# An attention and MLP kernel whose MLP blocks grow from three token tiles to four, with a split at the start of a block

## The chip, the core and the metric

The kernel runs on one core of a Trainium2 chip. The metric is the device time of one execution in microseconds (us). Before the change it is 976.59 us, the median of three runs (975.79 to 978.5). The engines are PE (matmuls), DVE (VectorE), ACT (ScalarE), POOL (GpSimd) and SP, which here issues transfers.

## The reference

Eight batches of eight heads, 512 local and 32 global tokens of 64 numbers each. A global token attends to all 544, a local one to the 32 global tokens and to the local ones within 32 positions. The result, 4352 tokens of 512 numbers, goes through an MLP of 2048 hidden numbers, all in float32:

```
s_g = scale * q_g @ k_all.T;  out_g = sm(s_g) @ v_all
s_ll = where(|i - j| <= 32, scale * q_l @ k_l.T, -1e9)
a_l = sm(concat([scale * q_l @ k_g.T, s_ll]));  out_l = a_l @ concat([v_g, v_l])
x = concat([out_g, out_l]) as tokens x 512
h = x @ w_in;  g = h / (1 + exp(-h));  out = g @ w_out
```

## The kernel before

The tokens form 34 tiles of 128. An attention **step** is one of 128 pairs of heads with one of 32 local tiles: four steps make a tile. A step loads queries and keys (`st_load`, into one of two `raw` buffers), splits them into a high part in float32r and a rest (`st_split`: an ACT cast and two DVE subtractions), multiplies them (`st_scores`, L363 and L364 of the profile, four matmuls of 224 columns into one PSUM bank), takes the softmax on DVE and ACT, takes the halves of the words apart on POOL (`st_halves`, L393), sends them to DRAM (`st_away`, L398) and brings them back transposed (`st_back`, L402). SP issues its transfers in order, so a transpose that waits for its data in DRAM holds up what stands behind it. For four steps together, `st_out` (L444) multiplies with the values into two banks, and the result is split into `xh` and `xl`, 256 columns at a time. Per batch there are four pairs of global heads: `g_load`, `g_split`, `g_scores` (L272, L273: two banks; then an ACT copy, L274, and a DVE sum, L275), `g_soft`, and `g_turn` (L309, L312: transposes `gt` and `gu`, copied by ACT at L310 and L315).

The MLP takes the tiles in **blocks**, `SIZES`: ten of three tiles and two of two. For each of sixteen slices `f` of the hidden numbers, `first_layer` does twelve matmuls over all tokens of the block (`h`, L600), as `w_hi` with `xh`, `w_hi` with `xl`, `w_lo` with `xh`; then tanh (ACT, L607), a product (DVE, L608), a cast to `gh` (ACT, L610) and the rest `gl` (DVE, L611). `second_layer` for the slice before (L627) does three matmuls of 512 columns per tile into banks `out`, one bank for each tile.

Order: on PE it is written out. A list of attention pieces, each with a due time in units of steps (`DUE`, `DMAT`, `HEAD`, `TURN`, `VLOADS`), is sorted, and `fill` releases the pieces that are due while the MLP runs: after each first layer as many shares as the block has tiles, then one after every three matmuls of the second layer. During block n the attention of block n + 1 is done. On the other engines a scheduler orders the work at build time; instructions in `hold` keep the program's order.

PSUM has eight banks: two for `h`, three for `out`, and three through which scores, global scores, transposes and attention outputs rotate in turn (`attbank`). A bank is written again when the engines that read it have done so.

Of the kernel before, what the change touches and what calls it, by code (L numbers as in the profile page):

```python
# [38 lines left out]
SIZES = (3,) * 10 + (2, 2)  # L39
# [32 lines left out]
def attention_moe_kernel(ctx: ExitStack, tc: tile.TileContext, qk0_in, qk_in, v_in, gqk, wts, out):  # L72
# [16 lines left out]
    def attbank(kind, name):  # L89
        if early:  # L90
            i = next(banks[kind]) % {"s": 3, "t": 2, "o": 3}[kind]
            if i and kind == "s":
                return ps_h.tile([P, 512], F32, tag="h", name=name)
            if i:
                return ps_out.tile([P, 512], F32, tag="out2" if kind == "t" else f"out{i - 1}", name=name)
# [329 lines left out]
    def st_out(k0, n, b, c, t):  # L425
        blk, i = block_of[t]
        xh, xl = xtiles(blk)
# [18 lines left out]
        for i, o in enumerate(banks_):  # L446
            m = min(2, n)
            prs = slice(k0 % NPR + 2 * i, k0 % NPR + 2 * i + m)
            o = o[:, : m * wide].rearrange("p (r q) -> p r q", r=m)
            hi = xh[:, prs, sl]  # L450
            nc.scalar.copy(out=hi, in_=o[:, :, :P])
            nc.vector.tensor_tensor(out=xl[:, prs, sl], in0=o[:, :, :P], in1=hi.bitcast(F32), op=ALU.subtract)
            if k0 >= NPR:
                gdst = acc[:, prs, SG * (b % 4) : SG * (b % 4 + 1)]
                if c == 0 and k0 >= NST:
                    nc.vector.tensor_copy(out=gdst, in_=o[:, :, P:])
                else:
                    nc.vector.tensor_tensor(out=gdst, in0=o[:, :, P:], in1=gdst, op=ALU.add)
# [14 lines left out]
    def g_tile(t):  # L473
        n, i = block_of[t]
        xh, xl = xtiles(n)
        sl = slice(i * P, (i + 1) * P)
        nc.scalar.copy(out=xh[:, :, sl], in_=acc)
        nc.vector.tensor_tensor(out=xl[:, :, sl], in0=acc, in1=xh[:, :, sl].bitcast(F32), op=ALU.subtract)
# [23 lines left out]
    AHEAD = NPR  # L502
    for k, (t, b, c, pr) in enumerate(steps):
# [30 lines left out]
        put(at + due["load"], st_load, *a)  # L534
# [44 lines left out]
    def fill(part):  # L579
# [3 lines left out]
        total = NF * SIZES[n] + (NF - 1) * SIZES[n] + (SIZES[n - 1] if n else 0)  # L583
# [9 lines left out]
    def first_layer(n, f):  # L593
# [4 lines left out]
        for wt, x in ((w_hi[f], xh), (w_hi[f], xl), (w_lo[f], xh)):  # L598
            for c in range(NCC):
# [7 lines left out]
        nc.scalar.activation(t[:, :nt], h[:, :nt], AF.Tanh, scale=0.5)  # L607
        nc.vector.scalar_tensor_tensor(out=t[:, :nt], in0=t[:, :nt], scalar=1.0, in1=h[:, :nt], op0=ALU.add,  # L608
                                       op1=ALU.mult)
        nc.scalar.copy(out=gh[:, :nt], in_=t[:, :nt])  # L610
        nc.vector.tensor_tensor(out=gl[:, :nt], in0=t[:, :nt], in1=gh[:, :nt].bitcast(F32), op=ALU.subtract)  # L611
        return gh, gl

    def second_layer(n, f, gh, gl):
# [10 lines left out]
        for done_, (i, j) in enumerate(order_, 1):  # L625
# [26 lines left out]
    for n in range(len(SIZES)):  # L652
        for f in range(NF):
# [7 lines left out]
            elif f == 0:  # L661
                advance(ends[n])
# [6 lines left out]
    second_layer(*pend)  # L669
# [69 lines left out]
```

## Time and profile before

| what | value |
|---|---|
| median of three runs | 976.59 us |
| the profiled execution | 978.29 us |
| its span, first to last instruction | 976.5 us |
| mean granted PE clock | 0.996 |
| start of the first MLP block | 47.9 us |
| starts of the blocks 1, 2, 3 | 141.9, 225.8, 314.1 us |
| starts of the last two blocks | 876.5, 925.3 us |

A row of a timeline gives the start in the span, the busy time, engine, line, operation, output and inputs, shape and count; in brackets stand the idle time before it and what released it. A row of a group gives the count, then the busy time in all and the mean of one in ns, then the idle time before and its releasers. In a row of a stretch stand its length, then the busy time and the number of instructions of PE, PEld (weight loads), DVE, ACT and POOL, the granted clock, the share of the DMA engines and GB/s. PE's busy times overlap, since its matmuls are pipelined.

### The profile page before, as it was taken

Reading aid. Unit: us, or ns where it says so; the run is one execution under the profiler, and the core shown is the slowest. Engines: PE = TensorE matmul, PEld = TensorE weight load, DVE = VectorE, ACT = ScalarE, POOL = GpSimd, SP = SyncE. Lnnn points to the kernel's source line nnn. Section 1 sums busy time; section 2 is a strip of 40 time slices with the busy share of each in tenths; the row PEclk is TensorE's granted clock in tenths of the full one; section 3 lists DMA queues with packets and bytes.
Section 4 is the critical chain, followed back from the end, with each engine's and each line's share of the span. In section 5 each row is a group of like instructions: output and inputs, shape, how many; then the busy total and the mean of one; then the engine's idle time right before and its main releaser. Section 6 shows DMA issues by size and latency. Waiting matters only on the chain.

```text
span 976.5 us, 17412 instructions
## 1 busy us (share of the span) xinstructions
PE 949.8 (97%) x5774; PEld 848.3 (87%) x5774; DVE 626.5 (64%) x1893; ACT 580.5 (59%) x1486; POOL 201.4 (21%) x413
## 2 busy tenths in 40 slices
PE   8789999999999999999999999999999999999998
PEld 6579888998899989989899999989989899899897
DVE  5888977766666677656577567766677565453322
ACT  6878876665556656555566656666575665343332
POOL 2122232122221222112122222312222221120000
PEclk9999999999999999999999999999999999999999
DMA  9968967576565766534655676566665664433000
GB/s 302 392 194 210 280 160 205 151 168 173 147 167 155 198 153 179 166 93 110 187 158 159 147 213 173 144 193 153 167 186 152 161 163 141 121 90 87 1 22 22
DMA packets 189305, 157.32 MB, mean 161 GB/s; under 512 B 128672, under 2 KB 148640, under 8 KB 189216
## 3 DMA queue, kind: packets, MB, share of 16 engines
q1 hardware_dynamic: 184800, 148.28, 56.2%
q10 hardware_dynamic: 4416, 7.93, 2.3%
q8 instruction: 46, 0.75, 0.3%
q14 instruction: 43, 0.35, 0.1%
HBM read 86.44 MB, written 39.32 MB: 129 GB/s over the span
## 4 chain that ended last, share of the span: by engine, by line
PE 82%; ACT 6%; DVE 6%; DMA 4%; issue 1%; SPq 0%; ACTq 0%; POOL 0%; DVEq 0%
PE out L627 34%; PE h L600 34%; PE o L444 6%; DMA raw<-in_qk_dram 2%; PE s L363 2%; PE s L364 2%; DMA raw_g<-in_gqk_dram 2%; ACT probs L372 1%; PE s L361 1%; DVE w_lo L231 1%; DVE w L221 1%; PE gt L309 1%; DVE probs L368 1%; DVE gl L611 1%; PE gs L272 0%
## 5 line engine op out<-in xcount | busy, mean ns | idle before, releaser
L393 POOL COPY halves<-probs 128x512 uint16<-128x512 uint16 x232 | 152.7, 684 | 495.2 <-ACT probs L379 185.2
L607 ACT ACTIVATE t<-h 128x384 f32<-128x384 f32 (+1 forms) x192 | 90.6, 472 | 166.5 <-PE h L600 156.3
L608 DVE SCALAR_TENSOR_TENSOR t<-t,h 128x384 f32<-128x384 f32 (+1 forms) x192 | 101.6, 529 | 115.1 <-ACT t L607 114.3
L627 PE MATMUL out<-w_hi,gh 128*128 128x512 f32 x544 | 164.9, 402 | 3.0 <-ACT gh L610 2.9
L600 PE MATMUL h<-xh,w_hi 128*128 128x384 f32 (+1 forms) x768 | 161.1, 332 | 4.6 <-ACT w_hi L230 4.5
L627 PE MATMUL out<-w_hi,gl 128*128 128x512 f32 x544 | 162.0, 396 | 0.2 <-DVE gl L611 0.2
L627 PE MATMUL out<-w_lo,gh 128*128 128x512 f32 x544 | 161.7, 395 | 0.0
L600 PE MATMUL h<-xh,w_lo 128*128 128x384 f32 (+1 forms) x768 | 158.8, 328 | 0.1
L600 PE MATMUL h<-xl,w_hi 128*128 128x384 f32 (+1 forms) x768 | 158.8, 328 | 0.0
L372 ACT ACTIVATE probs<-probs,st 128x224 f32<-128x224 f32 x244 | 115.8, 475 | 60.4 <-DVE st L368 59.7
L600 PEld LDWEIGHTS h<-xh,w_hi 128*128 128x128 f32 x768 | 133.7, 189 | 19.8 <-ACT w_hi L230 6.3
L611 DVE TENSOR_TENSOR gl<-t,gh 128x384 fp32r<-128x384 f32 (+1 forms) x192 | 109.6, 571 | 43.5 <-ACT gh L610 39.1
L368 DVE CUSTOM_DVE_ANT_0 probs<-s,mask 128x224 f32<-128x224 f32 x244 | 85.8, 386 | 75.6 <-PE s L364 64.8
L600 PEld LDWEIGHTS h<-xl,w_hi 128*128 128x128 f32 x768 | 133.4, 189 | 0.0
L600 PEld LDWEIGHTS h<-xh,w_lo 128*128 128x128 f32 x768 | 131.8, 189 | 0.7 <-DVE w_lo L231 0.7
L610 ACT CAST gh<-t 128x384 fp32r<-128x384 f32 (+1 forms) x192 | 94.4, 492 | 53.5 <-DVE t L608 52.9
L627 PEld LDWEIGHTS out<-w_hi,gl 128*128 128x128 f32 x544 | 100.7, 189 | 23.1 <-DVE gl L611 1.3
L627 PEld LDWEIGHTS out<-w_lo,gh 128*128 128x128 f32 x544 | 100.7, 188 | 21.7 <-issue 0.6
L627 PEld LDWEIGHTS out<-w_hi,gh 128*128 128x128 f32 x544 | 93.6, 189 | 15.7 <-ACT gh L610 6.5
L345 ACT CAST qk<-raw 128x704 fp32r<-128x704 f32 x100 | 77.7, 777 | 28.3 <-DMA raw<-in_qk_dram 23.8
L346 DVE TENSOR_TENSOR klo<-raw,qk 128x448 fp32r<-128x448 f32 x100 | 65.3, 653 | 30.4 <-ACT qk L345 28.1
L379 ACT ACTIVATE probs<-probs,st 128x224 f32<-128x224 f32 x118 | 56.7, 481 | 32.4 <-DVE st L375 30.8
(95 smaller groups left out, 1066.0 us busy)
## 6 DMA issues: line engine op xcount, KB each, us to landing
raw<-in_qk_dram SPq DMA_DIRECT2D x100, 352.0 KB, 3.4
away<-halves SPq DMA_DIRECT2D x116, 256.0 KB, 2.7
vraw<-in_v_dram SPq DMA_DIRECT2D x30, 512.0 KB, 4.9
raw_w<-in_wts_dram SPq DMA_DIRECT2D x29, 512.0 KB, 6.7
raw_g<-in_gqk_dram SPq DMA_DIRECT2D x32, 304.0 KB, 4.6
out_dram<-o ACTq DMA_DIRECT2D x29, 256.0 KB, 3.6
raw<-in_qk_dram SPq DMA_DIRECT2D x28, 240.0 KB, 4.8
pt<-away SPq DMA_TRANSPOSE x116, 3.3
```

Source lines behind the costliest of these rows:

```text
L345: nc.scalar.copy(out=qk, in_=raw)
L346: nc.vector.tensor_tensor(out=klo[:, :KW], in0=raw[:, QW:], in1=qk[:, QW:].bitcast(F32), op=ALU.subtract)
L368: nc.vector.tensor_tensor_reduce(out=p[:, u, :W], in0=ss[u], in1=mask_of[c], scale=-SCALE, scalar=3.0e38, op0=ALU.add, op1=ALU.min, accum_ ...
L372: nc.scalar.activation(p[:, u, :W], p[:, u, :W], AF.Exp, bias=st[:, u : u + 1], scale=-1.0, accum_out=st[:, 2 + u : 3 + u])
L393: nc.gpsimd.tensor_copy(out=halves[:, :, u], in_=p[:, 2 * P * u : 2 * P * (u + 1)].bitcast(U16).rearrange("p (j h) -> p h j", h=2))
L444: nc.tensor.matmul(o[D * u : D * (u + 1), :m], vraw[:, a, u, :], pt[:, u, a, :m], start=(a == 0), stop=(a == 1))
L600: nc.tensor.matmul(h[:, :nt], wt[:, c * P : (c + 1) * P], x[:, c, :nt], start=(i == 0), stop=(i == 3 * NCC - 1))
L607: nc.scalar.activation(t[:, :nt], h[:, :nt], AF.Tanh, scale=0.5)
L608: nc.vector.scalar_tensor_tensor(out=t[:, :nt], in0=t[:, :nt], scalar=1.0, in1=h[:, :nt], op0=ALU.add, op1=ALU.mult)
L610: nc.scalar.copy(out=gh[:, :nt], in_=t[:, :nt])
L611: nc.vector.tensor_tensor(out=gl[:, :nt], in0=t[:, :nt], in1=gh[:, :nt].bitcast(F32), op=ALU.subtract)
L627: nc.tensor.matmul(outs[n][i], g[:, i * P : (i + 1) * P], w, start=(f == 0 and j == 0), stop=(f == NF - 1 and j == 2))
```

## The change

`SIZES` becomes two blocks of three tiles and seven of four. `out` has four banks, and attention's rotation two (`attbank`). From block 1 on, `st_out` and `g_tile` only copy into one buffer `xr` in float32; `split_x` makes `xh` and `xl` of a whole block, 512 columns at a time, after the last first layer of the block before, and by then all attention of the block must have been given out. `xh`, `xl`, `xr` and `gh` have one buffer each. In the first layer `w_lo` with `xh` comes second, and `w_hi` with `xl` third. `gh` and `gl` are made by `parts`, which `second_layer` calls when its own matmuls with `gh` are done. The load of a step is due no later than 1.36 units after the step three before it, the global heads begin one step later in a batch, and the load of values is due 0.4 units later.

```diff
-SIZES = (3,) * 10 + (2, 2)
+SIZES = (3, 3) + (4,) * 7
+NT = max(SIZES)
-VLOADS = (None, -0.6, -1.0, 2.0)
+VLOADS = (None, -0.6, -1.0, 2.4)
+BEFORE = 1.36
-HEADS0, HEADS = (11, 1), (7, 2)
+HEADS0, HEADS = (11, 1), (8, 2)
...
-            kind = "sto"[next(banks["s"]) % 3]
+            kind = "so"[next(banks["s"]) % 2]
...
-            hi = xh[:, prs, sl]
-            nc.scalar.copy(out=hi, in_=o[:, :, :P])
-            nc.vector.tensor_tensor(out=xl[:, prs, sl], in0=o[:, :, :P], in1=hi.bitcast(F32), op=ALU.subtract)
+            if blk:
+                nc.scalar.copy(out=xwhole(blk)[:, prs, sl], in_=o[:, :, :P])
...
+    def split_x(n):
+        xr, nt = xraw.pop(n), SIZES[n] * P
+        xh, xl = xtiles(n)
+        for c in range(NCC):
+            nc.scalar.copy(out=xh[:, c, :nt], in_=xr[:, c, :nt])
+            nc.vector.tensor_tensor(out=xl[:, c, :nt], in0=xr[:, c, :nt], in1=xh[:, c, :nt].bitcast(F32),
+                                    op=ALU.subtract)
...
-        put(at + due["load"], st_load, *a)
+        ats.append(at)
+        put(min(at + due["load"], ats[k - 3] + BEFORE) if k >= ND + 3 else at + due["load"], st_load, *a)
...
-        total = NF * SIZES[n] + (NF - 1) * SIZES[n] + (SIZES[n - 1] if n else 0)
+        total = (2 * NF - 3) * SIZES[n] + (SIZES[n - 1] if n else 0)
...
-        for wt, x in ((w_hi[f], xh), (w_hi[f], xl), (w_lo[f], xh)):
+        for wt, x in ((w_hi[f], xh), (w_lo[f], xh), (w_hi[f], xl)):
...
+    def parts(n, f, t):
+        nt = SIZES[n] * P
+        gh = two.tile([P, NT * P], F32R, tag="gh", bufs=1, name=f"gh{n}_{f}")
+        gl = two.tile([P, NT * P], F32R, tag="gl", name=f"gl{n}_{f}")
         nc.scalar.copy(out=gh[:, :nt], in_=t[:, :nt])
         nc.vector.tensor_tensor(out=gl[:, :nt], in0=t[:, :nt], in1=gh[:, :nt].bitcast(F32), op=ALU.subtract)
...
+            if then and done_ == (2 * SIZES[n] if f < NF - 1 else 3 * SIZES[n] - 1):
+                then = parts(*then)
...
-            g = first_layer(n, f)
+            t = first_layer(n, f)
+            if f == NF - 1 and n + 1 < len(SIZES):
+                advance(ends[n + 1])
+                split_x(n + 1)
             fill(SIZES[n])
-            if pend is not None:
-                second_layer(*pend)
-            pend = (n, f, *g)
+            pend = second_layer(*pend, (n, f, t)) if pend else parts(n, f, t)
```

The first place is PE at the second pair of global heads of batch 5 (`gs_5_1`). Before, these rows stand there; in brackets are the engines whose signals a row waits for:

```order
L627 MATMUL out_0_5629<-w_hi_819,gh_3_5725 128x512 [waits Activation_49]
L627 MATMUL out_1_5630<-w_hi_819,gh_3_5725 128x512
L627 MATMUL out_2_5631<-w_hi_819,gh_3_5725 128x512
L272 MATMUL gs_5_1_5826<-qk_g_1_5766 128x272 [waits DVE_49]
L273 MATMUL gs_5_1_5826<-klo_g_1_5767,qk_g_1_5766 128x272
L272 MATMUL gs_5_1_5831<-qk_g_1_5766 128x272 [waits DVE_49,PE_49]
L273 MATMUL gs_5_1_5831<-klo_g_1_5767,qk_g_1_5766 128x272
L627 MATMUL out_0_5629<-w_lo_820,gh_3_5725 128x512
```

Now the head stands straight behind a first layer, and a step's scores `s` three matmuls of `out` behind it:

```order
L619 MATMUL h_4_5470<-xl_5138,w_hi_881 128x512 x4
L276 MATMUL gs_5_1_5490<-qk_g_1_5452 128x272 [waits DVE_49,PE_49,Activation_49]
L277 MATMUL gs_5_1_5490<-klo_g_1_5453,qk_g_1_5452 128x272
L276 MATMUL gs_5_1_5495<-qk_g_1_5452 128x272 [waits DVE_49]
L277 MATMUL gs_5_1_5495<-klo_g_1_5453,qk_g_1_5452 128x272
L649 MATMUL out_0_5264<-w_hi_819,gh_3_5459 128x512 [waits Activation_49]
L649 MATMUL out_1_5265<-w_hi_819,gh_3_5459 128x512
L649 MATMUL out_2_5266<-w_hi_819,gh_3_5459 128x512
L367 MATMUL s_5518<-qk_5500 128x224 [waits DVE_49]
```

The head takes both of attention's banks, so the last row waits for DVE's sum of the head's first bank. Heads with scores so close behind them, after a first layer, stand in ten places: one in block 3 and three each in blocks 4, 5 and 6. What stands on ACT at this head now (`t` is the tanh, `pg` the head's copies, `qk` the cast of a later load):

```order
L632 CAST gh_3_5459<-t_3_5415 128x512 [waits PE_49]
L383 ACTIVATE probs_85<-probs_85,st_5436 128x224 [waits DVE_49,Activation_49]
L623 ACTIVATE t_4_5483<-h_4_5470 128x512 [waits DVE_49,PE_49]
L278 COPY pg_127<-gs_5_1_5490 64x272 [waits PE_49]
L278 COPY pg_127<-gs_5_1_5495 64x272 [waits PE_49]
L349 CAST qk_5566<-raw_5465 128x704 [waits DMAHW4_49]
```

The copies stand behind the tanh of the first layer ahead of them, and on DVE the sums likewise behind the product. The second place is SP at the third pair of heads of batch 4. Before:

```order
L398 DMA away_4408<-halves_4356 128x1024 [waits Pool_49]
L238 DMA raw_g_2_4428<-in_gqk_dram 128x608 [waits DMAHW1_49,DVE_49,Activation_49]
L402 DMA_TRANSPOSE pt_130<-away_4408 128x4x256 [waits DMAHW6_49,DMAHW0_49]
L325 DMA raw_4462<-in_qk_dram 128x704 [waits DMAHW3_49,DVE_49,Activation_49]
L398 DMA away_4487<-halves_4464 128x1024 [waits Pool_49]
L325 DMA raw_4521<-in_qk_dram 128x704 [waits DMAHW7_49,DVE_49,Activation_49]
L402 DMA_TRANSPOSE pt_131<-away_4487 128x4x256 [waits DMAHW4_49,DMAHW2_49]
```

And now:

```order
L402 DMA away_4222<-halves_4172 128x1024 [waits Pool_49]
L329 DMA raw_4249<-in_qk_dram 128x704 [waits DMAHW3_49,DMAHW7_49,DVE_49,Activation_49]
L242 DMA raw_g_2_4251<-in_gqk_dram 128x608 [waits DMAHW4_49,DVE_49,Activation_49]
L406 DMA_TRANSPOSE pt_131<-away_4222 128x4x256 [waits DMAHW5_49,DMAHW2_49]
L402 DMA away_4308<-halves_4285 128x1024 [waits DMAHW6_49,Pool_49]
L329 DMA raw_4342<-in_qk_dram 128x704 [waits DMAHW4_49,DMAHW7_49,DVE_49,Activation_49]
L406 DMA_TRANSPOSE pt_132<-away_4308 128x4x256 [waits DMAHW6_49,DMAHW0_49]
```

A load of queries and keys that stood behind the transpose now stands in front of it, and each gap between two transposes has one. The third place is PE in block 1, at the second transposes of batch 2 (`gt_1`), now:

```order
L619 MATMUL h_7_2324<-xl_1777,w_hi_1120 128x384 x4
L313 MATMUL gt_1_2342<-ident,pg_128 128x128 [waits PE_49]
L313 MATMUL gt_1_2342<-ident,pg_128 128x128 x3
L316 MATMUL gu_1_2348<-ident,pg_128 32x128 [waits DVE_49]
L447 MATMUL o_2357<-pt_129,vraw_2100 64x160 [waits DMAHW5_49,DMAHW7_49,Activation_49,Pool_49]
L447 MATMUL o_2357<-pt_129,vraw_2100 64x160 x3
```

Behind `gt` and `gu`, in the two banks, `o` waits for ACT's copy of `gt`; before, a third bank stood free for it. In block 2 a piece of the same kind stands once more.

More of the change, by code (lines that the diff above doesn't have):

```diff
@@ L93, in attbank @@
                 return ps_h.tile([P, 512], F32, tag="h", name=name)
+            if kind == "t":
+                return ps_out.tile([P, 512], F32, tag=f"out{2 + i}", name=name)
             if i:
-                return ps_out.tile([P, 512], F32, tag="out2" if kind == "t" else f"out{i - 1}", name=name)
+                return ps_out.tile([P, 512], F32, tag=f"out{i - 1}", name=name)
         else:
-            kind = "sto"[next(banks["s"]) % 3]
+            kind = "so"[next(banks["s"]) % 2]
         return ps_att.tile([P, 512], F32, tag=f"att{kind}", name=name)
@@ L426, in st_out @@
         blk, i = block_of[t]
-        xh, xl = xtiles(blk)
         sl = slice(i * P, (i + 1) * P)
@@ L449, in st_out @@
             o = o[:, : m * wide].rearrange("p (r q) -> p r q", r=m)
-            hi = xh[:, prs, sl]
-            nc.scalar.copy(out=hi, in_=o[:, :, :P])
-            nc.vector.tensor_tensor(out=xl[:, prs, sl], in0=o[:, :, :P], in1=hi.bitcast(F32), op=ALU.subtract)
+            if blk:
+                nc.scalar.copy(out=xwhole(blk)[:, prs, sl], in_=o[:, :, :P])
+            else:
+                xh, xl = xtiles(0)
+                hi = xh[:, prs, sl]
+                nc.scalar.copy(out=hi, in_=o[:, :, :P])
+                nc.vector.tensor_tensor(out=xl[:, prs, sl], in0=o[:, :, :P], in1=hi.bitcast(F32), op=ALU.subtract)
             if k0 >= NPR:
@@ L474, in g_tile @@
         n, i = block_of[t]
[L475 to L478, printed above, removed]
+        nc.scalar.copy(out=xwhole(n)[:, :, i * P : (i + 1) * P], in_=acc)
     order = []
@@ L487, in attention_moe_kernel, with xwhole @@
     steps = [(t, b, c, pr) for t, (kind, b, c) in enumerate(order) if kind == "l" for pr in range(NPR)]
-    xblk = {}
+    xblk, xraw = {}, {}
     def xtiles(n):
         if n not in xblk:
-            xblk[n] = tuple(work.tile([P, NPR, 3 * P], F32R, tag=f"x{j}{n % 2}", name=f"x{j}_{n}") for j in "hl")
+            xblk[n] = tuple(work.tile([P, NPR, NT * P], F32R, tag=f"x{j}", name=f"x{j}_{n}") for j in "hl")
         return xblk[n]
+    def xwhole(n):
+        if n not in xraw:
+            xraw[n] = work.tile([P, NPR, NT * P], F32, tag="xr", name=f"xr_{n}")
+        return xraw[n]
+    def split_x(n):
[5 more added lines that the diff above has]
+                                    op=ALU.subtract)
     stream, marks = [], {}
@@ L502, in attention_moe_kernel @@
     AHEAD = NPR
+    ats = []
     for k, (t, b, c, pr) in enumerate(steps):
@@ L602, in first_layer @@
                 i += 1
-        t = two.tile([P, 3 * P], F32, tag="t", bufs=1, name=f"t{n}_{f}")
-        gh = two.tile([P, 3 * P], F32R, tag="gh", name=f"gh{n}_{f}")
-        gl = two.tile([P, 3 * P], F32R, tag="gl", name=f"gl{n}_{f}")
+        t = two.tile([P, NT * P], F32, tag="t", bufs=1, name=f"t{n}_{f}")
         nc.scalar.activation(t[:, :nt], h[:, :nt], AF.Tanh, scale=0.5)
@@ L647, in second_layer @@
                 nc.scalar.dma_start(out=out[r : r + np_, :], in_=sb)
+        return then
     advance(ends[0])
```

10 lines of the change are left out of this document (5 added, 5 removed).

## The prediction

> **What bounds the kernel now.** I read the page's busy shares and its chain first, then the PE timeline in a quiet stretch, then every gap of PE.
>
> ```profile
> span 976.5 us, 17412 instructions
> PE 949.8 (97%) x5774; PEld 848.3 (87%) x5774; DVE 626.5 (64%) x1893; ACT 580.5 (59%) x1486; POOL 201.4 (21%) x413
> PE out L627 34%; PE h L600 34%; PE o L444 6%; DMA raw<-in_qk_dram 2%; PE s L363 2%; PE s L364 2%; DMA raw_g<-in_gqk_dram 2%; ACT probs L372 1%; PE s L361 1%; DVE w_lo L231 1%; DVE w L221 1%; PE gt L309 1%; DVE probs L368 1%; DVE gl L611 1%; PE gs L272 0%
> ```
>
> PE is the bound, and two thirds of the chain are the two matmul layers of the MLP. So a change has only two ways to count: the distance between starts of successive matmuls, and the few places where PE waits. Matmuls overlap, so I take distances from starts, in a stretch with attention and in the last block without any:
>
> ```profile
> 501.57 0.85 PE L627 MATMUL out<-w_hi,gh 128*128 128x512 f32 x3
> 503.62 0.86 PE L600 MATMUL h<-xh,w_hi 128*128 128x384 f32 x4
> 505.72 0.26 PE L363 MATMUL s<-qk 128*128 128x224 f32 x1
> 930.91 0.64 PE L600 MATMUL h<-xh,w_hi 128*128 128x256 f32 x4
> 932.34 0.63 PE L627 MATMUL out<-w_hi,gh 128*128 128x512 f32 x2
> 933.73 0.64 PE L600 MATMUL h<-xh,w_hi 128*128 128x256 f32 x4
> ```
>
> Nine `out` matmuls stand between 501.57 and 503.62: 227.8 ns each. Twelve `h` matmuls of 384 columns between 503.62 and 505.72: 175.0 ns. Twelve of 256 columns between 930.91 and 932.34: 119.2 ns. Six `out` between 932.34 and 933.73: 231.7 ns.
>
> **Term 1, fewer and wider first-layer matmuls.** Before, ten blocks of three tiles and two of two give 1920 matmuls of 384 columns and 384 of 256: 1920 x 0.1750 + 384 x 0.1192 = 381.8 us. After, two blocks of three and seven of four give 384 of 384 columns and 1344 of 512. No `h` of 512 columns is in this trace. The step from 256 to 384 columns is 55.8 ns; one more step gives 230.8 ns, between the two figures of `out`, which is as wide. After: 384 x 0.1750 + 1344 x 0.2308 = 377.4 us. **-4.4 us**, and by the two `out` figures -8.4 (227.8) to -3.2 (231.7). The second layer keeps its 1632 matmuls.
>
> The rows say that a matmul costs its columns and some 12 ns more. The Trainium skill, "TensorE: Matmul & The Clock Gate", section "Wait — 56ns, not 53.3ns?", gives a warm matmul N / 2.4 GHz and about 2.5 ns; an estimate by it is 576 matmuls fewer x 2.5 ns, a gain of 1.4 us, and the sum below would end 3 us higher. The trace does not agree at these shapes (119.2 ns, where the rule gives 109), so the rows decide.
>
> **Term 2, loads in front of the waiting transposes.** Where PE waits longest after the first block, a load was late:
>
> ```profile
> 229.69 1.29 SPq L402 DMA_TRANSPOSE pt<-away  x1
> 231.15 0.46 SPq L325 DMA_DIRECT2D raw<-in_qk_dram  x1
> 238.81 0.34 PE L363 MATMUL s<-qk 128*128 128x224 f32 x1 [1.49 <-DVE qk L347]
> 244.63 1.23 SPq L402 DMA_TRANSPOSE pt<-away  x1
> 247.18 0.36 SPq L325 DMA_DIRECT2D raw<-in_qk_dram  x1
> 250.32 0.78 ACT L345 CAST qk<-raw 128x704 fp32r<-128x704 f32 x1 [2.48 <-PE o L444]
> 253.91 0.37 PE L272 MATMUL gs<-qk_g 128*128 128x272 f32 x1 [2.33 <-DVE acc L458]
> 254.24 1.39 PE L627 MATMUL out<-w_lo,gh 128*128 128x512 f32 x3
> 255.43 1.48 PE L627 MATMUL out<-w_hi,gl 128*128 128x512 f32 x3
> ```
>
> Both times the load of queries and keys went out behind a transpose that had waited in SP's queue. At 250.32 ACT had stood 2.48 us at the cast of that load, with the eviction of `o` behind it, so DVE's `acc` was late and PE stood 2.33 us; the release named is an older one. After that idle the clock was halved for a window: the rows at 254.24 and 255.43 are busy 1.39 and 1.48 us where such a row takes 0.85. These are the steps around the four global heads, where the new `min` in the load's due time bites (elsewhere it leaves the order as it was). I cost the removal at 1.49 + 2.33 + 0.54 + 0.63 = **-5.0 us**; the other end is 0, if the loads now wait in SP for their two buffers and the transposes behind them are late instead. How much room the transposes have is looked at in term 5.
>
> **Term 3, two banks where there were three.** `out` now takes four PSUM banks, so scores, global scores, transposes and attention outputs rotate through two. The order puts, ten times in blocks 3 to 6, a global head (two banks) straight behind a first layer, then three `out` matmuls, then the scores of a step, which take the head's first bank. The same head is in the trace, also straight behind a first layer, but with a third bank to follow:
>
> ```profile
> 510.37 0.28 PE L272 MATMUL gs<-qk_g 128*128 128x272 f32 x1
> 510.87 0.86 PE L627 MATMUL out<-w_hi,gh 128*128 128x512 f32 x3
> 510.57 0.49 ACT L607 ACTIVATE t<-h 128x384 f32<-128x384 f32 x1 [0.17 <-PE h L600]
> 511.09 0.67 ACT L274 COPY pg<-gs 64x272 f32<-64x272 f32 x2
> 511.09 0.55 DVE L608 SCALAR_TENSOR_TENSOR t<-t,h 128x384 f32<-128x384 f32 x1 [0.57 <-ACT t L607]
> 511.57 0.77 DVE L275 TENSOR_TENSOR pg<-gs,pg 64x272 f32<-64x272 f32 x2
> L607 ACT ACTIVATE t<-h 128x384 f32<-128x384 f32 x160 | 78.3, 489 | 121.9 <-PE h L600 111.7 <-DVE gl L611 8.4 <-DVE st L374 1.1
> L607 ACT ACTIVATE t<-h 128x256 f32<-128x256 f32 x32 | 12.3, 384 | 44.6 <-PE h L600 44.6
> L608 DVE SCALAR_TENSOR_TENSOR t<-t,h 128x384 f32<-128x384 f32 x160 | 88.2, 551 | 70.5 <-ACT t L607 69.7
> L608 DVE SCALAR_TENSOR_TENSOR t<-t,h 128x256 f32<-128x256 f32 x32 | 13.5, 421 | 44.6 <-ACT t L607 44.6
> ```
>
> The head starts at 0 (510.37). ACT's tanh goes first, then its two copies, then DVE's product and its two sums; the first sum ends about 0.43 us after 511.57, so the bank was free at 1.63 us. With 512 columns the tanh grows by 105 ns and the product by 130 ns (489 against 384 and 551 against 421, one step more): 1.87 us. The next scores want that bank at 0.50 + 3 x 0.23 = 1.19 us. Each of the ten waits 0.7 us: **+7 us**. Bounds: without tanh and product ahead the bank would be free at 1.3 us (0.25 for its two matmuls, 0.2 until ACT starts, then a copy of 0.38 and a sum of 0.43), 0.1 us late, +1; with one more operation of half a us ahead, +12.
>
> The Trainium skill, "Perfetto Trace Analysis", section "Optimizing Tensor Performance", says that independent matmul groups should rotate through different PSUM banks, so that one's evacuation overlaps the next one's matmuls. That speaks against this change, and the rows above are its price here; with three banks the row at 510.87 and those behind it have no idle time.
>
> **Term 4, transposes and order.** Twice (blocks 1 and 2) the transposes of `gt` stand behind a first layer with `o` straight behind them, in a bank that ACT must copy first:
>
> ```profile
> L310 ACT COPY pgt<-gt 128x512 f32<-128x512 f32 x16 | 9.3, 582 | 2.0 <-PE gt L309 2.0
> 128.27 0.87 PE L600 MATMUL h<-xl,w_hi 128*128 128x384 f32 x4
> 129.27 0.96 PE L600 MATMUL h<-xh,w_lo 128*128 128x384 f32 x4
> 134.51 0.98 PE L600 MATMUL h<-xh,w_hi 128*128 128x384 f32 x4 [1.44 <-ACT w_hi L230]
> 135.03 0.67 DVE L231 TENSOR_TENSOR w_lo<-w,w_hi 128x512 fp32r<-128x512 f32 x1
> ```
>
> A copy of 0.58 us behind a start of 0.2 us, with PE there 0.1 us after: 0.8 us each, **+1.6 us** (0 to 2.5). In the first block, `w_lo` is now wanted four matmuls (0.7 us) earlier: at 129.27 PE already waited 0.3 us for it and would wait 1.0; at 134.51 it would come to `w_lo` at 135.2, which is ready at 135.7. **+1.1 us** (0 to 2).
>
> **Term 5, the pace of block 1.** A block now carries the attention of the next one, and block 1 (three tiles) carries that of four:
>
> ```profile
> 142.00:226.00 84.00, 83.42 (x509) 75.38 (x508) 57.76 (x174) 53.57 (x136) 19.46 (x39) 1.00 0.65 167
> L393 POOL COPY halves<-probs 128x512 uint16<-128x512 uint16 x232 | 152.7, 684 | 495.2 <-ACT probs L379 185.2
> L372 ACT ACTIVATE probs<-probs,st 128x224 f32<-128x224 f32 x244 | 115.8, 475 | 60.4 <-DVE st L368 59.7
> L368 DVE CUSTOM_DVE_ANT_0 probs<-s,mask 128x224 f32<-128x224 f32 x244 | 85.8, 386 | 75.6 <-PE s L364 64.8
> away<-halves SPq DMA_DIRECT2D x116, 256.0 KB, 2.7
> pt<-away SPq DMA_TRANSPOSE x116, 3.3
> ```
>
> Block 1 took 84 us for twelve steps, 7.0 us each, with DMA at 0.65. By the pitches above, two tiles of the new block 1 have only 19 us of matmuls between their `o`, 4.4 us for each unit of the plan. Scores come 2.7 units ahead of `o`: 12 us, where it was 17 or more. From scores to landed transposes the rows give 0.4 + 2 x 0.39 + 2 x 0.48 + 0.5 + 2 x 0.68 + 2.7 + 3.3 = 10 us with no queueing at all. I take **+1 us**, between 0 and 6 (3 us on each of two tiles).
>
> **Costed at nothing.** The split at the start of a block: ACT's four casts (about 0.6 us each) and DVE's four subtractions start when the last first layer of the old block lets go of `xh`, and the next first layer is 12 `out` matmuls (2.8 us) and four `h` away; if ACT came there 1 us late, each of eight starts would cost that. One `gh` buffer: its cast waits for two thirds of the second layer before and has four more `out` and a whole first layer, 3.7 us, until it is read. The evictions of `o` lose a DVE subtraction each, which the split puts back.
>
> **The sum.** -4.4 - 5.0 + 7 + 1.6 + 1.1 + 1 = +1.3 us on the profiled execution of 978.29 us (span 976.5 and 1.8 around it): 979.6. That execution is 1.7 us over the median of the runs, 976.59, so I forecast **978 us**.
>
> **The rivals.**
> Faster: the bank waits are not paid. Mechanism: PE is late already when it gets to a tight pair, or ACT and DVE have their MLP part done, so 0.2 us is left of each 0.7. Term 3 falls to +2, term 4's `gt` to 0, and the forecast to 971. For it: DVE and ACT are busy for 58 and 54 of the 84 us in the row above. Against it: tanh and product stand ahead of the copies in all ten places.
> Slower: the pace of block 1 decides. Mechanism: transposes land after PE gets to `o`; the point is 12 us from scores to `o`, against 10 us and the queueing. With 3 us on each of two tiles the time is 983; the halved clock after such an idle (0.5 us a row above) would add to it.
> The loads do not do what is meant: SP waits for a free load buffer instead, term 2 is 0, and the time is 983.
>
> **How the numbers follow.** The forecast's case has 0.38, with 973.7 to 981 as its own range; the faster rival 0.32; block 1 0.18; the loads 0.12. About 0.3% (2.9 us) is what a measurement of this kernel can tell from no change, so the borders are 973.7 and 979.5. Faster: 0.32 and 0.03 of the forecast's case. Same: 0.30 of it and 0.02 of the loads. Slower: the rest, 0.33. All bounds at once would reach from 964 to 996; eight in ten lie between 967 and 986.
>
> **What would show it.** Starts of `h` with 512 columns 231 ns apart (term 1); no wait of PE behind a late `raw` near a global head, and a clock without that half window (term 2); ten waits of 0.7 us at scores, released by DVE's sum `pg` (term 3); a wait at `o` released by ACT's `pgt` in blocks 1 and 2 (term 4); transposes landing less than 1 us before `o` in block 1 (term 5). The prediction is wrong if `h` costs its columns alone, if PE waits at the starts of blocks, or if the waits on banks are missing.

## The result and the profile after

The changed kernel takes **986.88 us** (median of 6 runs, 984.39 to 993.93), the kernel before 976.75 beside it (6 runs): a ratio of 1.0115, 95% interval 1.0078 to 1.0151. It is slower by 10 us, and the forecast of 978 us and its range to 986 both miss.

The page of the changed kernel, the lines that answer to the first ones of before:

```profile
span 985.4 us, 16053 instructions
PE 945.9 (96%) x5198; PEld 786.6 (80%) x5198; DVE 618.3 (63%) x1769; ACT 581.4 (59%) x1422; POOL 204.3 (21%) x413
```

The span is 8.9 us longer, but PE is busy 3.9 us less. So the matmuls did get cheaper, and more than that was lost in waits. These are the two profiled executions, and in each the granted clock falls to half for windows of 3.4 us: four times in the changed kernel, twice before, at 1.7 us of lost clock each. So up to 3.4 of the 8.9 us are such windows. The timeline of PE in a quiet stretch (start, duration, work):

```profile
466.01 1.07 PE L619 MATMUL h<-xh,w_hi 128*128 128x512 f32 x4
...
468.73 0.84 PE L649 MATMUL out<-w_hi,gh 128*128 128x512 f32 x3
469.41 0.26 PE L367 MATMUL s<-qk 128*128 128x224 f32 x1
...
934.09 1.09 PE L619 MATMUL h<-xh,w_hi 128*128 128x512 f32 x4
935.02 1.08 PE L619 MATMUL h<-xh,w_lo 128*128 128x512 f32 x4
```

Twelve `h` of 512 columns between 466.01 and 468.73 are 226.7 ns apart, in the last block 232 ns. Summed over all starts, with waits of over 150 ns taken out, the first layer falls from 387.0 to 377.4 us (-9.6), the second from 382.2 to 380.0 (-2.2). The waits of PE by what ended them (total, times, longest), after and then before:

```profile
PE s L367 <- DVE pg L279: 8.4, 11, 2.0
PE s L367 <- DVE qk L351: 5.9, 5, 1.5
PE o L447 <- DMA pt<-away: 3.3, 2, 3.0
PE gs L276 <- DVE qk_g L253: 2.4, 2, 1.9
PE out L649 <- ACT gh L632: 2.0, 1, 2.0
```
```profile
PE h L600 <- ACT w_hi L230: 4.5, 3, 2.3
PE out L627 <- ACT gh L610: 2.9, 5, 1.5
PE gs L272 <- DVE acc L458: 2.3, 1, 2.3
PE s L361 <- DMA raw<-in_qk_dram: 2.2, 1, 2.2
PE s L363 <- DVE qk L347: 1.5, 1, 1.5
```

New or longer are the waits for a bank (`pg`) and those for the split of queries and keys (`qk`, `qk_g`). Where they lie is told by the stretches of blocks 0 and 1 (cut at the first `h` of each block; columns: length, busy time of PE, PEld, DVE, ACT, POOL, clock, DMA share, GB/s), after and then before:

```profile
49.60:144.60 95.00, 88.67 (x496) 78.24 (x495) 83.19 (x224) 76.75 (x199) 27.13 (x43) 0.96 0.79 218
144.60:246.60 102.00, 90.93 (x556) 79.92 (x555) 70.54 (x210) 63.21 (x164) 26.17 (x50) 0.98 0.68 183
```
```profile
47.90:141.85 93.95, 87.76 (x495) 77.20 (x494) 81.41 (x226) 75.64 (x193) 24.63 (x41) 0.98 0.78 213
141.85:225.80 83.95, 83.37 (x508) 75.32 (x507) 57.89 (x175) 53.37 (x136) 19.46 (x39) 1.00 0.65 168
```

Block 1 is the place: 11 us of 102 without PE at work, 0.6 of 84 before. These are its waits:

```profile
PE s L367 <- DVE qk L351: 5.9, 5, 1.5
PE s L367 <- DVE pg L279: 2.0, 1, 2.0
PE gs L276 <- DVE qk_g L253: 1.9, 1, 1.9
PE o L447 <- issue: 0.9, 1, 0.9
PE o L447 <- DVE st L372: 0.4, 1, 0.4
```

Measured from start to start, as the prediction does it, each wait is some 0.2 us longer than the idle time in the profile, since a matmul's busy time overlaps the next one's; the nine waits of over 150 ns are then 12.6 us, and the one before 0.7. Block 1 now does 16 steps of attention beside three tiles, for which PE has some 88 us of work by the distances between its starts. ACT and DVE are idle for a third of it, so neither is simply full. What happens is seen from one scores to the next, in the timeline of the changed kernel (in brackets the idle time before, and what ended it):

```profile
204.98 0.34 PE L367 MATMUL s<-qk 128*128 128x224 f32 x1 [0.86 <-DVE qk L351]
206.11 0.39 DVE L372 CUSTOM_DVE_ANT_0 probs<-s,mask 128x224 f32<-128x224 f32 x1
206.23 0.48 ACT L376 ACTIVATE probs<-probs,st 128x224 f32<-128x224 f32 x1 [1.53 <-DVE st L372]
206.71 0.47 ACT L376 ACTIVATE probs<-probs,st 128x224 f32<-128x224 f32 x1
207.18 0.50 ACT L632 CAST gh<-t 128x384 fp32r<-128x384 f32 x1
207.77 0.48 ACT L383 ACTIVATE probs<-probs,st 128x224 f32<-128x224 f32 x1
208.16 0.76 ACT L349 CAST qk<-raw 128x704 fp32r<-128x704 f32 x1
208.95 1.07 DVE L350 TENSOR_TENSOR klo<-raw,qk 128x448 fp32r<-128x448 f32 x1 [0.44 <-ACT qk L349]
210.03 0.42 DVE L351 TENSOR_TENSOR qk<-raw,qk 64x256 fp32r<-64x256 f32 x1
210.60 0.34 PE L367 MATMUL s<-qk 128*128 128x224 f32 x1 [0.75 <-DVE qk L351]
```

Scores, exponentials, norm, then in the same ACT queue the cast of the **next** step, its split on DVE, the next scores: a loop of 5.62 us, in which PE has 4.87 us of its own work. ACT had stood idle for 1.53 us ahead of the exponentials, with the cast behind them.

### The profile page after: what moved, and what is told of

It is laid out like the page before. It is cut to its first block, busy times and chain, and to the rows that moved or that the text cites. A ratio compares the mean times of both kernels' runs of the same rounds, so it can differ in the third digit from the quotient of the medians.

```text
span 985.4 us, 16053 instructions
## 1 busy us (share of the span) xinstructions
PE 945.9 (96%) x5198; PEld 786.6 (80%) x5198; DVE 618.3 (63%) x1769; ACT 581.4 (59%) x1422; POOL 204.3 (21%) x413
## 4 chain that ended last, share of the span: by engine, by line
PE 71%; DVE 2%; ACT 1%; issue 0%; ACTq 0%; DVEq 0%
PE out L649 30%; PE h L619 30%; PE o L447 5%; PE s L367 2%; PE s L368 2%; DVE t L624 1%; ACT t L623 1%; DVE pg L279 0%; PE gt L313 0%; PE gs L276 0%; PE gs L277 0%; DVE probs L372 0%; ACT o L661 0%; PE gu L316 0%; ACT pg L295 0%
## 5 line engine op out<-in xcount | busy, mean ns | idle before, releaser
L623 ACT ACTIVATE t<-h 128x512 f32<-128x512 f32 (+1 forms) x144 | 82.2, 571 | 172.9 <-PE h L619 165.1
L624 DVE SCALAR_TENSOR_TENSOR t<-t,h 128x512 f32<-128x512 f32 (+1 forms) x144 | 94.3, 655 | 118.6 <-ACT t L623 118.1
L376 ACT ACTIVATE probs<-probs,st 128x224 f32<-128x224 f32 x244 | 115.8, 476 | 62.8 <-DVE st L372 62.6
L619 PE MATMUL h<-xh,w_hi 128*128 128x512 f32 (+1 forms) x576 | 150.3, 383 | 0.0
L619 PE MATMUL h<-xh,w_lo 128*128 128x512 f32 (+1 forms) x576 | 148.4, 379 | 0.0
L619 PE MATMUL h<-xl,w_hi 128*128 128x512 f32 (+1 forms) x576 | 147.8, 378 | 0.0
L633 DVE TENSOR_TENSOR gl<-t,gh 128x512 fp32r<-128x512 f32 (+1 forms) x144 | 100.2, 696 | 54.5 <-ACT gh L632 53.2
L632 ACT CAST gh<-t 128x512 fp32r<-128x512 f32 (+1 forms) x144 | 85.5, 594 | 80.1 <-PE out L649 59.9
L619 PEld LDWEIGHTS h<-xh,w_hi 128*128 128x128 f32 x576 | 106.1, 189 | 20.8 <-issue 1.8
L447 PE MATMUL o<-pt,vraw 128*64 128x160 f32 x960 | 69.1, 295 | 6.2 <-DMA pt<-away 3.3
```

The source lines that it names most:

```text
L376: nc.scalar.activation(p[:, u, :W], p[:, u, :W], AF.Exp, bias=st[:, u : u + 1], scale=-1.0, accum_out=st[:, 2 + u : 3 + u])
L447: nc.tensor.matmul(o[D * u : D * (u + 1), :m], vraw[:, a, u, :], pt[:, u, a, :m], start=(a == 0), stop=(a == 1))
L619: nc.tensor.matmul(h[:, :nt], wt[:, c * P : (c + 1) * P], x[:, c, :nt], start=(i == 0), stop=(i == 3 * NCC - 1))
```

## The experiments

Each ratio is to the kernel before, run on the same chip; 95% interval in brackets.

| run | us | ratio |
|---|---|---|
| e1 casts written earlier | 987.52 | 1.0104 [1.0082, 1.0126] |
| e2 global heads earlier | 988.21 | 1.0122 [1.0100, 1.0144] |
| e3 before, two banks | 997.93 | 1.0217 [1.0191, 1.0242] |
| e4 four tiles from block 6 | 980.52 | 1.0033 [1.0017, 1.0048] |
| e5 casts ahead of exponentials | 982.29 | 1.0040 [1.0024, 1.0055] |
| e6 third bank, blocks 0 and 1 | 989.56 | 1.0117 [1.0099, 1.0135] |
| e7 e4 with a third bank | 979.96 | 1.0023 [1.0011, 1.0036] |
| e8 without the load rule | 989.46 | 1.0113 [1.0095, 1.0131] |
| e9 four tiles from tile 15 | 974.36 | 0.9965 [0.9949, 0.9982] |
| e10 e5, late heads earlier | 975.53 | 0.9975 [0.9959, 0.9992] |
| e11 sizes of before | 978.01 | 1.0004 [0.9986, 1.0023] |
| e12 before, load rule | 972.71 | 0.9944 [0.9925, 0.9964] |
| e13 e3, heads one step later | 992.50 | 1.0153 [1.0137, 1.0169] |
| e14 e9, outputs moved | 983.13 | 1.0057 [1.0043, 1.0072] |
| e15 e14, third bank | 976.80 | 0.9996 [0.9984, 1.0009] |
| e16 e9, third bank, transposes | 969.79 | 0.9915 [0.9893, 0.9937] |
| e17 e9, slower pace in block 0 | 977.92 | 1.0001 [0.9984, 1.0019] |
| e18 e16, old order of products | 969.60 | 0.9921 [0.9905, 0.9936] |

**Block 1: e1, e5, e6.** The first try put the casts earlier in the program:

```diff
+        if 28 <= k < 41:
+            due["split"] = -1.05
```

> The changed kernel, with the cast of queries and keys of steps 28 to 40 written half a step earlier. TensorE's order is that of the changed kernel, row for row; on ScalarE the casts of steps 33 to 42 then stand ahead of the exponentials of the step before, where the changed kernel has them behind. Theory (the loop of block 1: scores, exponentials, cast of the next step, next scores, is longer than TensorE's work between two scores): the waits of over 150 ns in block 1, 12.6 us together, fall to 4 us or less, and the time from 986.9 to about 978 us. Rival (loads: the transfer of queries and keys lands too late whatever stands in ScalarE's queue, since SyncE waits 24 and 36 us for buffers): the cast waits for its transfer instead, and the time stays within 2 us of 986.9. Second rival (ScalarE has simply too much to do in block 1): the wait moves to the exponentials or the tanh, and less than 3 us are won.

The order on ACT did not change: the builder puts each engine's queue in order by what it takes to be ready first, so ACT's casts stayed behind the exponentials, contrary to what I had written. From 186 us on, where they should have moved, the trace has them at the same places to 0.2 us. So this run tested nothing. The second run pins the order:

```diff
-        if 28 <= k < 41:
+        if 28 <= k < 43:
...
-            nc.scalar.activation(p[:, u, :W], p[:, u, :W], AF.Exp, ...
+            e = nc.scalar.activation(p[:, u, :W], p[:, u, :W], AF.Exp, ...
+            if 32 <= k < 43:
+                hold(e)
```

> The kernel of the first run (casts of steps 28 to 42 written half a step earlier), and the exponentials of steps 32 to 42 kept behind what is written ahead of them on ScalarE; the first run left ScalarE's order as it was, this one puts the casts of steps 33, 35 to 40 and 42 ahead of the exponentials of the step before. TensorE's and SyncE's orders are those of the changed kernel. Theory (loop of block 1 through the cast): the six waits for the split of about 1 to 1.5 us between 184 and 232 us go, block 1 is 6 us shorter, the time is about 981 us. Rival (the transfers land too late, or ScalarE has too much to do): the casts now wait for their transfer with the exponentials behind them, and the time stays within 2 us of 987 or rises.

982.29 us; against the changed kernel 5 us less by the medians, 7 by the ratios. In the profiled executions 5.1 us of it lie in block 1. The timeline of this run, two steps on:

```profile
196.26 0.26 PE L367 MATMUL s<-qk 128*128 128x224 f32 x1
198.03 0.78 ACT L349 CAST qk<-raw 128x704 fp32r<-128x704 f32 x1
198.71 0.48 ACT L376 ACTIVATE probs<-probs,st 128x224 f32<-128x224 f32 x1
199.48 0.42 DVE L351 TENSOR_TENSOR qk<-raw,qk 64x256 fp32r<-64x256 f32 x1
200.18 0.27 PE L367 MATMUL s<-qk 128*128 128x224 f32 x1
204.78 0.26 PE L367 MATMUL s<-qk 128*128 128x224 f32 x1
```

The cast stands ahead of the exponentials, the split is done 0.3 us before PE wants it, and PE goes from scores to scores without idling. The stretch of block 1, and its wait for the split, which was 5.9 us:

```profile
140.90:237.80 96.90, 90.58 (x556) 79.92 (x555) 68.31 (x210) 63.15 (x164) 24.43 (x51) 0.98 0.75 196
```
```profile
PE s L367 <- DVE qk L351: 1.4, 2, 1.0
```

So the loop through the cast is shown, and with it 5 of the 18 us that block 1 had lost or taken on (102.0 against 84.0). The bank and the global head's split keep their waits (1.9 and 1.5 us). The rival was that the loads come too late: of the casts from 193 to 218 us that now stand ahead, none waited for its load; the one at 229 us did, for 1.31 us. e6 asks whether banks make block 1 slow; three output tiles leave the fourth tile's bank free in blocks 0 and 1:

```diff
-            kind = "so"[next(banks["s"]) % 2]
+            i = next(banks["s"]) % (3 if now[0] < 2 else 2)
+            if i == 2:
+                return ps_out.tile([P, 512], F32, tag="out3", name=name)
+            kind = "so"[i]
```

> The changed kernel, with a third bank in turn for the attention while blocks 0 and 1 run (these have three output tiles, so that the bank of the fourth is free until block 2). TensorE's order stays. Theory (two banks cost most in blocks 0 and 1, where ScalarE and VectorE empty a bank late; two banks alone had made the kernel before 20 us slower, 7 and 4 us of it in blocks 0 and 1): block 0 comes back to 92 to 94 us and block 1 to 97 to 99, the time is 976 to 980 us. Rival (what is lost in block 1 is the loop of casts and scores, to which banks are nothing): block 1 keeps 10 us or more of waits, and the time is 984 to 987 us.

It won nothing; in block 1 no wait for `pg` is left, but the wait for the split is longer:

```profile
PE s L370 <- DVE qk L354: 8.6, 7, 1.9
```

**The step from three tiles to four: e4, e7, e9, e11.** These change the sizes:

```diff
-SIZES = (3, 3) + (4,) * 7
+SIZES = (3,) * 6 + (4,) * 4          # e4, e7
+SIZES = (3,) * 5 + (4,) * 4 + (3,)   # e9
+SIZES = (3,) * 10 + (2, 2)           # e11, with NT = 4
```

> The changed kernel with block sizes 3, 3, 3, 3, 3, 3, 4, 4, 4, 4 in place of 3, 3, 4, 4, 4, 4, 4, 4, 4: the step from three tiles to four lies between blocks 5 and 6 in place of blocks 1 and 2. Theory (a block of three tiles that carries the attention of four has too little TensorE work for each step): block 1 loses under 4 us to waits of over 150 ns, block 5 loses 8 us or more, and the time is 987 to 990 us, some 2 us of it for the 12 tiles that stand in blocks of three again. Rival (it belongs to block 1: first steps with split queries, weights, first global scores): block 1 keeps 9 us or more of waits, block 5 has under 4.

The loss moved with the step, though it is smaller than the 8 us expected: block 5 has 5.8 us of waits, block 1 1.9. The stretches of blocks 1 and 5 of e4, and the wait for the split in block 5:

```profile
142.50:227.80 85.30, 83.37 (x508) 75.05 (x507) 57.91 (x177) 54.96 (x142) 18.66 (x40) 1.00 0.66 169
469.20:565.10 95.90, 90.12 (x555) 79.02 (x554) 66.43 (x212) 62.32 (x164) 26.39 (x52) 0.98 0.72 187
```
```profile
PE s L367 <- DVE qk L351: 3.2, 3, 1.8
```

The other 2.6 us of block 5 are waits for the bank `pg`. Block 5 takes 95.9 us where block 1 had taken 102: 16 steps beside three tiles cost 6 us less there, so 980.5 us came out and not the 987 of the theory. In the trace about half of the casts there (8 of 15) start behind the exponentials of the step before, where it is 13 of 15 in block 1 of the changed kernel. e9 avoids 16 steps beside three tiles altogether:

> The changed kernel with block sizes 3, 3, 3, 3, 3, 4, 4, 4, 4, 3. The step from three tiles to four now falls on the block that holds tile 16, a tile of global rows with no attention steps of its own: block 4 has three tiles of TensorE work and 12 steps, like every block of three before it, in place of 16. Theory (what costs is 16 steps beside three tiles): no block loses more than 4 us to waits after block 0, and against 980.5 us for the sizes 3 (six times), 4 (four times) the time falls by 5 to 8 us to 973 to 976 us, at or below the kernel before. Rival (any block of four beside two banks costs it): 979 us or more.

974.36 us, as the theory had it. Block 4, which leads to the first block of four tiles, has 12 steps:

```profile
393.40:476.20 82.80, 81.98 (x500) 73.61 (x499) 53.16 (x163) 51.63 (x132) 18.65 (x37) 1.00 0.64 167
```

It loses 0.8 us. With a third bank as well (e6's edit, up to block 5), e4 stays where it is: its block 5 takes 99.0 us, 3 more, and there 13 of 15 casts start behind the exponentials.

> The kernel with the step from three tiles to four between blocks 5 and 6, and a third bank in turn while blocks 0 to 5 run. Theory (banks and the step to four tiles are two causes that add up): against that kernel's 980.5 us blocks 0 to 5 win 7 to 10 us, and the time is 970 to 974 us, below the kernel before. Rival (the third bank moves the wait to the next thing): 978 us or more.

> The changed kernel with the block sizes of before (3 ten times, then 2, 2): its two banks, loads, split at a block's start and order of matmuls stay. Theory (the step to four tiles costs 8 to 9 us, wider matmuls gain 9, two banks and the rest cost the net 10): without both the time is 984 to 988 us, about that of the changed kernel, with no block losing over 5 us to waits after block 0. Rival (all that was lost is lost by the blocks of four): 977 us or less.

e11, with everything but the sizes, stands level with the kernel before. My theory was 6 to 10 us too high: with the sizes of before, the two banks, the split and the rest cost about what the load rule gains (e12), 5 us, if the two simply add up. (Two banks alone cost the kernel before far more, e3 below; which of the other edits makes them cheap in e11 was not separated.) So the sizes, with the banks as they are, carry the whole loss of 9 to 11 us, although against e11 the wider matmuls make the first layer 7.3 and the second 1.6 us shorter (384.7 to 377.4, 381.6 to 380.0).

**Banks: e2, e10, e3, e13.**

```diff
-HEAD = dict(load=-0.9, split=0.2, scores=0.8, soft=1.0, slot=0.3)
+HEAD = dict(load=-0.9, split=0.0, scores=0.5, soft=1.0, slot=0.3)   # e2: all batches; e10: as LATE, for b > 2 only, on top of e5
```

> The changed kernel, with the split of the global keys written 0.2 and their scores 0.3 of a step earlier in blocks 1 to 7. By TensorE's order, re-uses of a bank with under 1.2 us of other work between them fall from 16 to 10: the ten pairs of global scores and next scores go, and four pairs of scores and global scores come. Theory (two banks: each such pair costs 0.7 to 0.8 us): ten waits of 0.8 go and up to four of about 0.7 come, the time falls by 5 us to about 982. Rival (the wait is for VectorE's turn, not for the bank, and comes back at the next place): within 2 us of 986.9.

> The kernel whose casts stand ahead of the exponentials in block 1 (982.3 us), with the global scores from the fourth batch on 0.3 and their split 0.2 of a step earlier. Theory (each of the ten waits at scores for the bank of the global scores costs 0.7 to 0.8 us, and what was won by this in blocks 3 to 6 had been lost again in blocks 1 and 2 when all batches were moved): blocks 3 to 6 are together 6 us shorter, as they were then, blocks 1 and 2 stay, and the time is 976 to 977 us. Rival: nothing is won, 981 us or more.

In e2 the rival held: blocks 4 to 6 each fell from 110.4 to 108.7 us, but blocks 1 and 2 rose by 3.0 and 1.5, and nothing was left. e10 moves only the late batches and wins 6 to 7 us over e5, as expected; in its blocks 3 to 8 no wait for `pg` is left. This is what such a wait looks like in the changed kernel, head, three `out`, next scores:

```profile
489.48 0.28 PE L276 MATMUL gs<-qk_g 128*128 128x272 f32 x1
489.99 0.86 PE L649 MATMUL out<-w_hi,gh 128*128 128x512 f32 x3
491.52 0.37 PE L367 MATMUL s<-qk 128*128 128x224 f32 x1 [0.67 <-DVE pg L279]
```

Two banks in the kernel before:

```diff
-            kind = "sto"[next(banks["s"]) % 3]
+            kind = "so"[next(banks["s"]) % 2]
...
-HEADS0, HEADS = (11, 1), (7, 2)
+HEADS0, HEADS = (11, 1), (8, 2)      # e13 only
```

> The kernel before, with two banks in turn for scores, global scores, outputs and global transposes from block 1 on, in place of three; nothing else. By TensorE's order there are 13 re-uses of a bank with under 1.3 us between them, where the kernel before has none. Theory (each costs what the like ones cost in the changed kernel, 0.7 to 1.1 us): 8 to 12 waits are new, and the time goes from 976.8 to about 985 us. Rival (the changed kernel's waits at scores come from its other order, and two banks alone suffice): within 2 us of 976.8.

> The kernel before with two banks in turn, and the global loads, splits and scores of each batch from the third on one step later (the changed kernel's place). Theory (with the old place, five outputs stand 0.9 us ahead of global scores in the same bank, and two banks are dear for that): the close pairs of outputs and global scores are gone, and the time falls from 997.9 to 985 us or less. Rival (two banks cost the same wherever the heads stand): 995 us or more.

Two banks cost that kernel 20 us, more than twice the theory. 7 us are in block 0. Blocks 3 and 5, 81.2 and 83.8 us before, take 84.6 and 88.4 in e3, and 80.4 and 82.5 in e13: the close pairs of outputs and heads were dear, and one step's shift takes that away. The whole wins only 5 to 6 us, since block 2 is 3.6 us longer than in e3 and block 0 keeps its 101 us. e13 lands between theory and rival; the rest of the 15 us isn't settled.

**Loads: e12 and e8.** One line each way (e12 also brings in `BEFORE` and the list `ats`):

```diff
-        put(at + due["load"], st_load, *a)
+        put(min(at + due["load"], ats[k - 3] + BEFORE) if k >= ND + 3 else at + due["load"], st_load, *a)
```

> The kernel before with the rule for the loads alone. Theory (the late loads at the scores behind the global part, 1.5 to 2.3 us in two places, are what the rule takes away): the time falls by 2 to 5 us to about 974. Rival (with two raw buffers the load cannot start earlier): within 1.5 us of 977.

> The changed kernel without its rule for the loads (each load of queries and keys where its own due time puts it, as before). Theory (the rule saves the late loads, 5 us): waits for a transfer at the scores behind the first split steps come back, some 2 to 3 us in each of one or two places from block 1 on, and the time rises by 4 to 5 us to about 991. Rival (two raw buffers set when a load can start, the rule only makes SyncE wait at them): within 1.5 us of 987.

In the kernel before the rule wins 5 us, and block 2 falls from 88.4 to 82.5 us. Taken out of the changed kernel, the median rises by 2.6 us and block 1 by 3.2, but the ratio does not move: undecided.

**Block 0 and the best version: e14 to e18.** In every kernel made from the changed one, e14 and e15 apart, PE waits 3.0 to 4.8 us for a transposed plane in block 0, the kernel before not at all. Here it is in the changed kernel, with the matmuls behind it at a clock of 0.5:

```profile
112.59 1.23 PE L447 MATMUL o<-pt,vraw 128*64 128x160 f32 x8 [3.04 <-DMA pt<-away]
...
115.11 1.33 PE L649 MATMUL out<-w_hi,gh 128*128 128x512 f32 x3
```

```diff
+        if k == 19:
+            due["out"] += 0.4             # e14, e15
...
-TURN1, TURN = (0.65, 1.5), (0.4, 1.5)
+TURN1, TURN = (0.65, 1.5), (0.4, 1.1)   # e15, e16, e18, with e6's third bank up to block 4
...
-        total = (2 * NF - 3) * SIZES[n] + ...
+        total = (2 * NF - (3 if n else 1)) * SIZES[n] + ...    # e17
...
-        for wt, x in ((w_hi[f], xh), (w_lo[f], xh), (w_hi[f], xl)):
+        for wt, x in ((w_hi[f], xh), (w_hi[f], xl), (w_lo[f], xh)):   # e18
```

> The kernel of block sizes 3 (five times), 4 (four times), 3 (974.4 us), with the four outputs of steps 16 to 19 written 0.4 of a step later. Theory (block 0 is longer because the work is spread over less of the block, and TensorE comes to these outputs 3 to 4 us before the last transposed plane lands): the wait at about 109 us goes, block 0 falls from 96.6 to about 93 us, and the time to about 971. Rival (the plane's transfer is held up by the weights, and TensorE stops at the next scores for theirs): block 0 stays above 95 us and the time within 1.5 us of 974.4.

> The kernel of the run above, with a third bank for the attention in blocks 0 to 4 and the second half of the global transposes of a batch 0.4 of a step earlier, so that they no longer stand right ahead of outputs in the same bank. By TensorE's order the re-uses of a bank with under 1.3 us between them fall from 15 to 4. Theory (each such wait costs 0.5 to 1.1 us): 5 us are won on the run above, to 966 to 968 us. Rival (the third bank wins nothing, as in the run with it in blocks 0 to 5): within 2 us of the run above.

In these two the outputs of step 16 come behind the write of step 20 into the same plane and are computed from that, so these kernels give another result; in e14 PE stood 11.95 us for it. They tell nothing of the question, and their times stand beside no other.

> The kernel of block sizes 3 (five times), 4 (four times), 3 (974.4 us), with a third bank for the attention in blocks 0 to 4 and the second half of a batch's global transposes 0.4 of a step earlier; the outputs of steps 16 to 19 stay in their place. By TensorE's order the re-uses of a bank with under 1.3 us between them fall from 15 to 4. Theory (each such wait costs 0.5 to 1.1 us): the waits at global transposes and outputs in blocks 5 to 7 (0.7 to 1.1 us, four times) and at scores in blocks 1 to 4 (about 0.5 us, four times) go, and the time falls by 4 to 6 us to 968 to 970 us. Rival (the third bank moves the waits to the next thing, as before): within 2 us of 974.4.

> The kernel of block sizes 3 (five times), 4 (four times), 3 (974.4 us), in which block 0 alone spreads its attention over 31 parts in place of 29, as the kernel before did. Theory (in block 0 the planes land just as TensorE reaches the outputs at 107 and 136 us, since the work comes 7 per cent faster): the wait of 3.5 us at 109 us falls to 1 us or less, block 0 from 96.6 to 93 us, and the time to about 971. Rival (two banks and the order of the weights make block 0 longer, the pace does not): block 0 stays above 95 us and the time within 1.5 us of 974.4.

> The kernel of 969.8 us (block sizes 3 five times, 4 four times, 3; third bank in blocks 0 to 4; global transposes earlier), with the low weights third in each hidden chunk again, as in the kernel before. Theory (in block 0 the low weights are split late, and wanting them second costs what the prediction put at 1.1 us): block 0 becomes 1 to 3 us shorter than 96.8 us, the time 967 to 969 us. Rival (block 0 is set by the planes that land at 109 and 138 us): block 0 stays within 1 us, the time within 1.5 us of 969.8.

e16 beats both kernels, as its theory had it: 969.79 us, 0.85% below the kernel before; the load rule alone wins 5 of these 8 us there (e12). Blocks 1 to 4 are together 3.6 us shorter than in e9, blocks 5 to 7 only 1.1. e17 falls the other way: block 0 takes 98.5 us, its wait for the plane is still 3.5 us, and block 1 grows to 89.2, so the pace alone is not the cause. e18 has a block 0 of 93.1 us in the one profiled execution (96.8 in e16's) and the same time: undecided, and the wait for the plane (3.3 us) stays. What makes block 0 longer stays open.

## Why the prediction was wrong

**Term 5 is the step that failed**: "I take +1 us, between 0 and 6 (3 us on each of two tiles)". From start to start, the waits of over 150 ns in block 1 went from 0.7 to 12.6 us, +11.9. The link was wrong as well as the size. I had followed the path behind the scores, to the transposes at `o`. In block 1 no matmul at `o` waited for a transpose: the last of each four landed 1.9, 1.9, 2.8 and 0.2 us before the matmul that reads it, the last of these close, as the term had feared. What came late was the path ahead of the scores: cast and split of the next step, which stand in ACT's queue behind this step's softmax. Their five waits are 6.7 of the 12.6 us; 2.0 are the split of a global head, 2.2 a bank at scores, 1.7 waits at `o`, of which 1.1 belong to term 4. e5 shows the queue: pinning the casts ahead takes those 6.7 us to 1.8. e4, where block 1 keeps 1.9 us of idle, and e9 show that nearly all of it comes with the step from three tiles to four; for the head's split and the bank the path was not tested by itself. The rival "the pace of block 1 decides" named the right block and the wrong mechanism.

**Term 1** was right in sign and too small: -9.6 us against -4.4, beyond its bound of -8.4. The sum for the changed kernel came out as forecast, 377.4 us. The sum before was too low, 381.8 against 387.0: the 175.0 ns for 384 columns came from one quiet slice, and over all 1920 such matmuls the mean is 177.7 ns, some of them in windows of half clock. With 512 columns the mean is 229 ns. The second layer's -2.2 us had no term.

**Term 2** held where it can be seen alone (-5 us in e12; forecast -5.0); in the changed kernel its worth is not settled (e8). The clock did not stay clear of half windows, as the prediction's sign had asked: there are four where there were two.

**Term 3** held: ten waits of 0.72 to 0.84 us between starts, 8.0 us against 7, and e10 wins 6 to 7 of them. The faster rival, that they are not paid, fell.

**Term 4**: 1.1 and 0.9 us at `o`, against 1.6. The profile does not name what released them, but ACT's copy of `gt` ends 0.1 us ahead of both. At `gu`, where the term had nothing, PE waited 0.6 us in block 2 and 1.2 in block 0, until DVE had read the scores that stood before. The price of the low weights (+1.1) is not measured alone (e18); no wait at `h` is among the changed kernel's waits, neither for weights nor at the start of a block.

Block 0 also began 1.7 us later in this execution, which was not in the sum; the runs made from the changed kernel have it anywhere from 47.7 to 50.7 us. With term 5 at its 1 us in place of 11.9 the changed kernel would stand at about 976 us, beside the forecast. That the other errors nearly cancel is luck: term 1 alone was 5 us off.

## What to carry to other kernels

When a block is made wider, look at the block that feeds it: its work per step shrinks, and the longest loop through an in-order queue (here exponentials, then the next step's cast) becomes the bound before any engine is full. Follow each step's inputs back as far as its outputs forward. Compare with the right kernel, too: against the old sizes with the same banks (e11, 978.0 us) wider blocks won 4 us once the step to them was placed where the feeding block had no extra steps (e9), and 2 to 3 once the loop was cut and the bank waits moved (e10). But the old kernel with the load rule alone takes 972.7 us (e12), less than either. Only e16 and e18 lie below that, by 3 us, and their intervals overlap with its own, so it is not shown that wider blocks pay against that kernel.

## What was not expected of the hardware

Some idle time of PE is paid twice. Two stretches of the changed kernel (the clock is the third figure from the end):

```profile
156.60:160.20 3.60, 3.60 (x13) 3.47 (x12) 2.13 (x9) 1.53 (x5) 0.59 (x1) 0.53 0.64 176
231.00:238.00 7.00, 5.13 (x29) 4.27 (x27) 5.50 (x14) 4.26 (x11) 1.56 (x2) 1.00 0.66 143
```

The clock is halved for 3.4 us in three places of blocks 0 and 1, and each time this begins 2.8 to 3.0 us after the start of an idle of 2.03, 3.04 or 2.01 us (at 54.7, 109.6 and 153.7); such a window costs up to 1.7 us. Behind the idle of 1.87 us at 231.6, and those of 1.3 to 1.5 us, there is none. The length of the idle does not decide it alone. e9 has no window behind an idle of 3.55 us at 109.6, though PE was busy less than a sixth of the stretch around it, and e4 has one behind 1.79 us at 544.7. This is e9 right behind its idle:

```profile
113.20:117.00 3.80, 3.80 (x23) 3.24 (x24) 1.83 (x9) 1.96 (x7) 0.24 (x1) 1.00 0.93 325
```

What else decides it stays open. Over the six runs of the changed kernel the time goes roughly with the mean clock: 984.39 us at 0.998, 984.53 at 0.996, 986.61 at 0.997, 987.15 at 0.993, 989.97 at 0.992, 993.93 at 0.990.
